# A long convolution's transform on one core: the product of u and D at the beginning of a block instead of behind the complex products

## The chip, the cores and the metric

The kernel runs on one core of one Trainium2 chip. The metric is the device time of one execution in microseconds (us); several executions are timed and the median counts. One further execution is profiled, and it has a time of its own. The engines have these names in the profile: PE is TensorE (PEld its weight loads), DVE is VectorE, ACT is ScalarE, POOL is GpSimd, and SP is the engine that here only issues transfers (DMA).

## The reference

Two independent layers read their own inputs, and their results stand side by side in the output (2048 x 2048, bf16). The left one is a recurrent attention with memory over 64 segments of 32 rows. The right one is a long convolution, and the change lies there:

```python
K = jnp.einsum('dn,dnl,dn->dl', Cc, P, dB).real          # P = exp(dt * A * l), complex
Kf = rfft(pad(K, L)); Uf = rfft(pad(u.T, L))             # L = 2048, transforms of length 4096, for each of 1024 channels
y = irfft(Uf * Kf)[:, :L].T + u * Dskip[None, None, :]
```

The last term, `u * Dskip`, is the product of the title; in the kernel it is one instruction for each sixteenth of the rows and channels.

## The kernel before

The work is in two parts. The convolution (`part_b`) runs first, up to about 593 us of the profile; the attention (`part_a`) follows. The second half of the convolution also loads the attention's weights, into memory that it gives up piece by piece.

Behind the tables, the convolution's transform is a loop of 16 blocks `b` (line 1526). Block `b` covers a quarter of the channels (`dq = b // 4`, DQ = 256 of them) and a quarter of the frequencies (`b % 4`). A block has these steps:

- VectorE, `times_u` (line 1380): four complex products of the spectrum of u, which SP has loaded as `uq` (the profile calls it wq), with the kernel's spectrum, which TensorE left in PSUM (`hps`). For each half n_ = 0, 1 it writes `Z` and then `Y`. `Zs` and `Yp` are one buffer each, used by every block.
- VectorE, `rotate` (lines 1383 and 1384): Y is completed from Z. From block 4 on there are two instructions for both halves (`whole`).
- VectorE, lines 1466 and 1467: `even` and `odd`, the sum and the difference of Y's halves. `even` is no buffer of its own, it is `Zs[:, 1]`, the Z of the second half; `odd` is called od in the profile.
- GpSimd, lines 1469, 1471 and 1472: from `even` (two instructions), and from `odd` (one each), the block's rows of `Bt`. In block 15 VectorE does lines 1471 and 1472.
- TensorE, `spectrum` (line 1224): the kernel's spectrum of block b + 1, 20 matmuls for each half. Three PSUM tiles go round, so that the second half's matmuls write the tile which the first half's products of block b have read.
- TensorE, from block 4 on, `inverses(b - 4, i)` (lines 1489 to 1521): the inverse transform of a pair of rows, 16 channel quarters in all, as matmuls of the matrices `MI` with `Bt`, and one matmul (line 1520) that adds the pair's product of u and D with the identity. ScalarE writes the result over the product (line 1521), and a transfer that ScalarE issues stores it (line 1493, issued during the inverses of the next pair).

The product itself is `skips(n_)` (line 1483), one VectorE instruction on 128 x 1024 bf16 (line 1486): `uu`, the pair's rows of u, times `Dsk`, D on all partitions, written over `uu`. The rows of pair n_ are loaded by `load_pair(n_)` (line 1481, SP), two blocks ahead of their use; pairs 0 and 1 are loaded in block 3. `load_u(b + 1)` (line 1215, SP) loads the spectrum of u for the next block, each half as soon as the products of that half are done.

`pointwise(b, ...)` is a generator: its first step issues `times_u`, its second the rest. Between the two stand, in the loop, the product, the loads and the spectra. Each engine runs its instructions in the order in which the program issues them; the engines wait for each other with semaphores. The loads and stores take their semaphores from a set of eight, in turn: a transfer is issued only when the one that last had its semaphore has landed. Which of them share one follows from the order that the framework gives the program.

The generator `residents` (line 1671) hands out the loads of the attention's weights: some in each block, and behind the loop the weights that go into the memory of `Zs`, `Yp`, the first `Bt` (given up by `ctx2.close()`, line 1591, ahead of the load of pair 15, line 1594), and of the matrices `MI`, one for each inverse that is done. The attention loads further pieces by itself, the first of them half of one query weight (a_half in the profile, line 352).

Of the kernel before, what the change touches and what calls it, by code (L numbers as in the profile page):

```python
# [711 lines left out]
def part_b(ctx, tc, u, A_re, A_im, B_re, B_im, C_re, C_im, log_dt, Dskip, out_b, ahead, copies, residents, first_state):  # L712
# [379 lines left out]
    def load_k(half, KT, lo):  # L1092
        n_ = KT.shape[1] // DH
        ks_ = [KT[:, DH * j:DH * j + DH] for j in range(n_)]
        for j, t_ in enumerate(ks_):
            c = lo + j
            src_ = Kp[half][8 * (c - 3):8 * (c - 2)] if c > 2 else Kx[half][4 * c:4 * c + 4, 8:40] if c < 2 else Kx[half][8:16, 8:40:2]
            sy.dma_start(out=t_, in_=src_ if c > 2 else src_.rearrange("i j g c -> i j (g c)"))
        return ks_
# [105 lines left out]
    def weighted(kc, n_, amp):  # L1205
        a_ = amp.rearrange("p (j q) -> p j q", j=3)[:, :, 256 * n_:256 * n_ + 256]
        g_ = G[kc][:, n_, 2:5].rearrange("p j s h f -> p j s (h f)")
        v.tensor_tensor(out=g_, in0=g_, in1=a_.unsqueeze(2).to_broadcast([128, 3, 2, 256]), op=ALU.mult)
# [4 lines left out]
    def load_u(b):  # L1213
        for n_ in range(2):
            sy.dma_start(out=uq[n_], in_=Ud[b % 4, b // 4][:, 2 * n_:2 * n_ + 2].rearrange("p a c d -> p (a c d)"))

    def spectrum(b, n_, outs, halves=(0, 1)):
        dq, kc = b // 4, b % 4
        KT = ks[dq // 2]
        d = slice(DQ * (dq % 2), DQ * (dq % 2) + DQ)  # L1220
        for half in halves:
            for cs in range(2):
                for j in range(5):
                    pe.matmul(outs[half][:, cs, :], lhsT=G[kc][:, n_, j, cs, half, :], rhs=KT[j][:, d], start=(j == 0), stop=(j == 4), skip_group_check=True)  # L1224
# [144 lines left out]
    def make(kc, n):  # L1369
        for _ in range(n):  # L1370
            next(made[kc])

    def halves():
        t_ = ps_e.tile([128, 2, 512], F32, name="pa", tag="pa")
        return [t_[:].rearrange("p h (c d) -> p h c d", c=2)]

    def times_u(s_, Y, Z, n_):
        us = uq[n_].rearrange("p (a c d) -> p a c d", a=2, c=2)
        for i, t_ in ((1, Z), (0, Y)):
            v.tensor_tensor(out=t_, in0=us[:, :, i, :].unsqueeze(2).to_broadcast([128, 2, 2, DQ]), in1=s_[n_][0], op=ALU.mult)  # L1380

    def rotate(Y, Z):
        v.tensor_tensor(out=Y[:, :, 0, :], in0=Y[:, :, 0, :], in1=Z[:, :, 1, :], op=ALU.subtract)
        v.tensor_tensor(out=Y[:, :, 1, :], in0=Y[:, :, 1, :], in1=Z[:, :, 0, :], op=ALU.add)
# [64 lines left out]
    def blocks(t_):  # L1449
        return t_.rearrange("p i c d -> p (i c) d")  # L1450

    def pointwise(b, s_):
        kc, Bt = b % 4, Bs[b // 4]
        Y = Yp[:] if b else first
        whole = b > 3
        if b:
            for n_ in range(2):
                times_u(s_, Y[:, n_], Zs[:, n_], n_)
                if n_ == 0 and not whole:
                    rotate(Y[:, n_], Zs[:, n_])  # L1460
        yield
        if whole:
            rotate(Y.rearrange("p n a c d -> p (n a) c d"), Zs[:].rearrange("p n a c d -> p (n a) c d"))
        elif b:
            rotate(Y[:, 1], Zs[:, 1])
        v.tensor_tensor(out=even, in0=Y[:, 0], in1=Y[:, 1], op=ALU.add)
        v.tensor_tensor(out=odd[:], in0=Y[:, 0], in1=Y[:, 1], op=ALU.subtract)
        for i, op in ((0, ALU.add), (1, ALU.subtract)):
            gp.tensor_tensor(out=Bt[:, kc, 0, i], in0=even[:, 0], in1=even[:, 1], op=op)
        eng, to = v if b == 15 else gp, blocks(Bt[:, kc, 1])  # L1470
        eng.tensor_tensor(out=to[:, 0:4:3], in0=odd[:, 0], in1=odd[:, 1, ::-1], op=ALU.add)
        eng.tensor_tensor(out=to[:, 2:0:-1], in0=odd[:, 0], in1=odd[:, 1, ::-1], op=ALU.subtract)
# [6 lines left out]
    def load_pair(n_, pool, bufs=4):  # L1479
        uu = held[n_] = pool.tile([128, 2, 2, DQ], BF16, name="uu", tag="uu", bufs=bufs)  # L1480
        sy.dma_start(out=uu[:].rearrange("p i a d -> p (i a) d"), in_=rows_of(u_v, n_))

    def skips(n_):
        d = slice(DQ * (n_ // 4), DQ * (n_ // 4) + DQ)
        uu = held[n_][:].rearrange("p i a d -> p (i a) d")
        v.tensor_tensor(out=uu, in0=uu, in1=Dsk[:, d].unsqueeze(1).to_broadcast([128, 4, DQ]), op=ALU.mult)

    def inverses(n_, i):
        while ended:
            ended.pop(0)()  # L1490
        inverse(n_ // 4, PAIRS[2 * n_ % 8 + i], held[n_][:, i])
        if i:
            ended.append(lambda: sc.dma_start(out=rows_of(out_v, n_), in_=held[n_][:].rearrange("p i a d -> p (i a) d")))
# [32 lines left out]
    for b in range(16):  # L1526
        dq = b // 4
        if b % 4 == 0:
            Bs[dq] = (bp0, bp)[dq % 2].tile([128, 4, 2, 2, 2, DQ], BF16, name="Bt", tag="B")
        points = pointwise(b, now)  # L1530
        next(points)
        if b >= 4:
            skips(b - 4)
        if 0 < b < 15:
            load_u(b + 1)
        if b >= 4:
            load_pair(b - 2, iv)
        if b == 3:
            v.tensor_scalar(out=ident[:], in0=ident[:], scalar1=float(PLEN / 2), scalar2=None, op0=ALU.mult)
            load_pair(0, iv)  # L1540
            load_pair(1, iv)
            ctx_p.close()
            ctx_k.close()
            ps_h = ctx.enter_context(tc.tile_pool(name="b_psh", bufs=3, space=PSUM))
            ps_y = ctx.enter_context(tc.tile_pool(name="b_psy", bufs=2, space=PSUM))
        if b == 0:
            now = nxt_
        elif b + 1 < 16:
            now = []
            for n_ in range(2):  # L1550
                if b < 3:
                    if n_:
                        next(points, None)
                    weighted(b + 1, n_, amps[b + 1])
                now.append(halves() if b < 3 else [ps_h.tile([128, 2, 2, DQ], F32, name="hps", tag="h")[:]])
                spectrum(b + 1, n_, [now[n_][0][:, half] for half in range(2)])
                if b == 1:
                    make(3, 7)
        next(points, None)
        if b < 4:  # L1560
            for i in (2 * b, 2 * b + 1):
                sy.dma_start(out=MI[i][:], in_=MId[2 * i:2 * i + 2].rearrange("c p a k q -> p c a k q"))
        if b == 2:
            rows4 = g0[0:4, 5120:6144]
            for i in range(4):
                for half in range(2):
                    sy.dma_start(out=rows4[i:i + 1, DH * half:DH * half + DH], in_=Kx[half][31:32, NF - 1].rearrange("i g c -> i (g c)"))
            sy.dma_start(out=w4, in_=u[0:4, :])
            gp.tensor_tensor(out=w4, in0=rows4[:, 0:D], in1=w4, op=ALU.mult)
            gp.memset(l4, 0.0)  # L1570
            gp.memset(l4[:, :, 127:128], float(PLEN / 2))
            gp.affine_select(out=l4[:, :, 127:128], in_=l4[:, :, 127:128], compare_op=ALU.is_ge, fill=0.0, base=0, pattern=[[1, 4], [0, 1]],
                             channel_multiplier=-1)
        for _ in range({1: 2, 2: 2, 3: 1, 4: 2, 5: 2, 6: 2, 7: 2, 11: 3, 12: 3, 13: 2, 14: 3, 15: 3}.get(b, 0)):
            next(resident)
        for _ in range(4 if b in (3, 4) else 0):
            second.pop(0)()
        if b == 5:
            ks.append(load_k(1, k1[:, 0:2560], 0))
        if b == 4:  # L1580
            state = first_state(g0[0:8, 5120:6144], iv.tile([128, 8, 24], BF16, name="xt0", bufs=1))
            next(state)
        if b == 10:
            state.send(ps_y.tile([128, 8, 128], BF16, name="yp", tag="yp")[:, :, 0:8])
        if b >= 4:
            for i in range(2):
                inverses(b - 4, i)
# [48 lines left out]
def kernel(  # L1636
# [90 lines left out]
    with ExitStack() as ctx_b:  # L1727
        part_b(ctx_b, tc, B_u[0], B_A_re, B_A_im, B_B_re, B_B_im, B_C_re, B_C_im, B_log_dt, B_Dskip, out_b, ahead, copies, residents, first_state)
# [37 lines left out]
```

## Time and profile before

| what | value |
|---|---|
| three executions | 1933.28, 1943.44, 1939.64 us; median 1939.64 |
| the profiled execution | 1942.13 us; span of its trace 1940.4 us |
| PE busy | 1783.4 us, 92% of the span |
| DVE busy | 1356.6 us, 70% |
| ACT busy | 918.6 us, 47% |
| POOL busy | 499.4 us, 26% |
| HBM read and written | 531.92 MB and 71.63 MB, 311 GB/s over the span |

By stage, busy time of the engines and mean share of the DMA engines:

| stage, us | length | PE | DVE | POOL | DMA share |
|---|---|---|---|---|---|
| 446 to 579, blocks 4 to 15 | 133 | 113.81 | 123.05 | 76.01 | 0.78 |
| 579 to 593, the last inverses | 14 | 13.31 | 2.25 | 8.62 | 0.98 |
| 593 to 640, the first segment and more | 47 | 27.83 | 16.39 | 2.81 | 1.02 |
| 640 to 1940, the other segments | 1300 | 1220.76 | 822.93 | 223.67 | 0.93 |

How to read it: the span is the time from the first to the last instruction of the profiled execution, and the execution's own time is 1.7 us longer. A busy share says nothing of what bounds a stage; that is seen where an engine waits and for whom. An instruction's length in the timeline includes the time in which it stands issued but is held up, so the same instruction can have two lengths. Instructions of one engine can overlap by some hundredths of a microsecond, so that the distance between starts is a better measure of what one costs than its length.

### The profile page before, as it was taken

The numbers are of one execution on the slowest core, as the hardware profiler recorded it, in microseconds if no ns is written. First come the engines' busy times: TensorE is split into PE (matmuls) and PEld (weight loads), VectorE is DVE, ScalarE is ACT, GpSimd is POOL, SyncE is SP. The second block draws the span as 40 slices with busy tenths as digits, with TensorE's granted clock in tenths as the row PEclk, the third lists the DMA queues.
The fourth block names the chain that finished last, engine by engine and source line by source line (L and its number), as shares of the span: only waits on it lengthen the run. The fifth ranks groups of instructions, "written<-read, shape, count | busy, mean of one in ns | idle before, by whom it ended". The sixth has DMA issues, their size and how long they took to land.

```text
span 1940.4 us, 73670 instructions
## 1 busy us (share of the span) xinstructions
PE 1783.4 (92%) x31563; PEld 1091.3 (56%) x31563; DVE 1356.6 (70%) x3357; ACT 918.6 (47%) x1654; POOL 499.4 (26%) x885
## 2 busy tenths in 40 slices
PE   8999999888886999999999999999999999999998
PEld 3666565556763555555555555555555555555554
DVE  8699999798992666676666666666667666766650
ACT  8799999850112343444444443434344444434420
POOL 2364545236561111111111111111112121111120
PEclk9999999868997999999999999999999999999999
DMA  7889898868699999999999999999999999999993
GB/s 222 250 238 282 238 282 250 216 193 249 196 294 373 334 336 341 339 342 342 340 339 349 344 335 340 346 339 344 331 349 343 343 343 357 336 337 339 345 338 96
DMA packets 341744, 594.21 MB, mean 306 GB/s; under 512 B 94100, under 2 KB 216476, under 8 KB 339368
## 3 DMA queue, kind: packets, MB, share of 16 engines
q1 hardware_dynamic: 297944, 534.99, 81.4%
q10 hardware_dynamic: 36816, 29.59, 4.8%
q0 software_dynamic: 6656, 24.92, 3.4%
q8 instruction: 247, 4.05, 0.8%
q14 instruction: 81, 0.66, 0.1%
HBM read 531.92 MB, written 71.63 MB: 311 GB/s over the span
## 4 chain that ended last, share of the span: by engine, by line
PE 46%; DMA 33%; DVE 12%; ACT 5%; issue 2%; POOL 1%; ACTq 0%; SPq 0%; POOLq 0%; DVEq 0%
PE acc L414 19%; DMA wst<-WD_v 12%; DMA wst<-WD_o 9%; PE pp L527 8%; DMA arena<-PKd 4%; PE pe L667 3%; DMA wst<-WD_k 3%; DMA wst<-WD_q 2%; PE tr L425 2%; PE pro L184 2%; PE yp L1508 1%; DVE nr L1269 1%; PE hps L1224 1%; PE pro L197 1%; PE pa L1224 1%
## 5 line engine op out<-in xcount | busy, mean ns | idle before, releaser
L414 PEld LDWEIGHTS <-a_hT 128*32 128x32 bf16 x12351 | 327.9, 96 | 331.5 <-issue 80.5
L420 ACT CAST arena<-acc 128x512 bf16<-128x512 f32 x384 | 224.8, 585 | 406.0 <-PE acc L414 336.8
L414 PE MATMUL acc<-wst,a_hT 128*32 128x512 bf16 x2308 | 230.5, 383 | 36.6 <-DMA wst<-WD_v 27.1
L527 PEld LDWEIGHTS <-arena 128*32 128x32 bf16 x8256 | 215.3, 96 | 76.7 <-issue 52.6
L428 POOL COPY arena<-arena 128x128 bf16<-128x128 bf16 x128 | 37.4, 292 | 707.1 <-DMA arena<-PKd 343.8
L335 DVE TENSOR_SCALAR arena<-keep 128x256 int32<-128x256 int32 x508 | 174.1, 394 | 26.6 <-PE acc L414 26.6
L414 PE MATMUL acc<-XM,a_hT 128*32 128x512 bf16 x2560 | 173.4, 381 | 0.0
L454 DVE TENSOR_REDUCE a_mx<-sc 128x4 f32<-128x160 f32 (+1 forms) x192 | 71.7, 374 | 80.9 <-PE sc L442 80.8
L197 PE MATMUL pro<-XM,wsl 128*128 128x512 bf16 x512 | 122.4, 382 | 4.0 <-DVE kst L206 2.2
L527 PE MATMUL pp<-W_o,arena 128*32 128x256 bf16 x3584 | 121.2, 273 | 1.3 <-issue 1.3
L414 PE MATMUL acc<-W,a_hT 128*32 128x512 bf16 x1536 | 119.7, 384 | 0.0
L544 DVE COPY arena<-tr 128x512 bf16<-128x512 bf16 x64 | 27.2, 424 | 129.2 <-PE tr L425 129.2
L458 ACT ACTIVATE sc<-sc 128x160 f32<-128x160 f32 (+1 forms) x192 | 63.9, 333 | 103.3 <-DVE sc L455 102.7
L462 DVE TENSOR_REDUCE a_mx<-sc 128x4 f32<-128x160 f32 (+1 forms) x192 | 72.8, 379 | 55.2 <-ACT sc L458 54.9
L489 POOL TENSOR_TENSOR arena<-arena,a_BD 128x128 bf16<-128x128 bf16 x128 | 51.0, 399 | 213.6 <-DVE arena L472 203.0
L1269 DVE TENSOR_SCALAR nr<-ptt 128x456 f32<-128x456 int16 x128 | 80.2, 627 | 30.4 <-PE ptt L1247 27.4
L1261 ACT ACTIVATE E<-pa 128x648 bf16<-128x648 f32 x128 | 87.6, 712 | 17.0 <-PE pa L1253 15.4
L414 PE MATMUL acc<-wq,a_hT 128*32 128x512 bf16 x1024 | 92.3, 383 | 0.0
L527 PE MATMUL pp<-wst,arena 128*32 128x256 bf16 x1536 | 76.2, 274 | 17.5 <-DMA wst<-WD_o 16.5
L414 PE MATMUL acc<-g,a_hT 128*32 128x512 bf16 x1024 | 91.2, 380 | 0.0
L623 ACT CAST arena<-pp 128x128 bf16<-128x128 f32 x64 | 17.0, 265 | 155.7 <-DVE arena L623 155.7
L513 ACT CAST arena<-pv 128x512 bf16<-128x512 f32 (+1 forms) x128 | 61.3, 479 | 60.3 <-PE pv L499 33.3
(342 smaller groups left out, 4001.7 us busy)
## 6 DMA issues: line engine op xcount, KB each, us to landing
wst<-WD_v SPq DMA_DIRECT2D x256, 512.0 KB
wst<-WD_k SPq DMA_DIRECT2D x192, 512.0 KB
wst<-WD_o SPq DMA_DIRECT2D x192, 512.0 KB
wst<-WD_q SPq DMA_DIRECT2D x128, 512.0 KB
Ud<-ux POOLq DMA_DIRECT2D x16, 1024.0 KB, 8.9
wq<-Ud SPq DMA_DIRECT2D x32, 512.0 KB
wsl<-in_A_Wk_dram SPq DMA_DIRECT2D x16, 512.0 KB
wsl<-in_A_Wv_dram SPq DMA_DIRECT2D x16, 512.0 KB
```

Of the source, the lines that this page charges most:

```text
L197: nc.tensor.matmul(a[:], lhsT=w[:, kc, 128 * j:128 * j + 128], rhs=xTl[:, kc, :, :].rearrange("p s k -> p (s k)"), start=(kc == 0), stop=( ...
L335: nc.vector.tensor_scalar(out=out.bitcast(I32), in0=in_.bitcast(I32), scalar1=0, scalar2=None, op0=ALU.bitwise_or)
L414: nc.tensor.matmul(a[32 * g:32 * g + 32, o_:o_ + rhs.shape[1]], lhsT=hT[:, kc, :], rhs=rhs, start=(kc == 0), stop=(kc == KC - 1), tile_pos ...
L420: nc.scalar.copy(out=q, in_=a[:])
L454: nc.vector.tensor_reduce(out=m_, in_=x, axis=AX.X, op=ALU.max)
L458: nc.scalar.activation(out=flat(sc, i), in_=flat(sc, i), func=ACT.Exp, scale=scale)
L462: nc.vector.tensor_reduce(out=m_, in_=x, axis=AX.X, op=ALU.add)
L513: copy(out=o[:, i:i + n], in_=p[:, i:i + n, :].rearrange("p a (g q) -> p a g q", g=4))
L527: nc.tensor.matmul(po[32 * qt:32 * qt + 32, o_:o_ + rhs.shape[1]], lhsT=oT[:, h % 4, (h % 16) // 4, :], rhs=rhs, start=False, stop=(h == 3 ...
L667: nc.tensor.matmul(pe[n][:], lhsT=left[2 * b + hi // 16][:, 128 * (hi % 16):128 * (hi % 16) + 128], rhs=wo[u][:, 1024 * hh + 512 * n:1024 ...
L1261: sc.activation(out=T["E", r, e // 4][:, lo:lo + 8 * NE].rearrange("p (i c) -> p i c", i=2), in_=T.pop(("p", r, e))[:, :, 0:4 * NE], func= ...
L1269: v.tensor_scalar(out=T["n", r, e // 4][:, lo:lo + 8 * NT], in0=T.pop(("t", r, e))[:, 0:8 * NT].bitcast(I16)[:, 0:16 * NT:2], scalar1=floa ...
```

## The change

`skips(b - 4)`, the product, is called before the generator's first step instead of behind it. On VectorE the twelve products of blocks 4 to 15 are thus issued ahead of the four instructions of `times_u`, which is directly behind `odd` of the block before (in block 11 one short copy stands between). The four products of the last pairs, behind the loop, stay.

```diff
         if b % 4 == 0:
             Bs[dq] = (bp0, bp)[dq % 2].tile([128, 4, 2, 2, 2, DQ], BF16, name="Bt", tag="B")
+        if b >= 4:
+            skips(b - 4)
         points = pointwise(b, now)
         next(points)
-        if b >= 4:
-            skips(b - 4)
         if 0 < b < 15:
             load_u(b + 1)
```

## The prediction

> **What bounds the kernel now.** I read the page's slices first, then the chain of waits, then the timeline of single engines in the stretch that the change touches.
>
> ```profile
> DVE  8699999798992666676666666666667666766650
> ```
>
> Slices are 48.5 us. The change lies in the sixteen blocks of the transform; those it touches (4 to 15) run from 446 to 579 us, slices 10 to 12, where VectorE has 8, 9, 9 tenths. Behind them come 64 segments of attention (593 us to the end), which it does not touch. One block, on VectorE and GpSimd:
>
> ```profile
> 503.74 1.22 DVE L1467 TENSOR_TENSOR od<-y 128x1024 f32<-128x1024 f32 x1
> 504.87 1.22 DVE L1380 TENSOR_TENSOR z<-wq,hps 128x1024 f32<-128x1024 f32 x1
> 506.00 1.22 DVE L1380 TENSOR_TENSOR y<-wq,hps 128x1024 f32<-128x1024 f32 x1
> 507.34 1.22 DVE L1380 TENSOR_TENSOR z<-wq,hps 128x1024 f32<-128x1024 f32 x1
> 508.48 1.21 DVE L1380 TENSOR_TENSOR y<-wq,hps 128x1024 f32<-128x1024 f32 x1
> 509.61 0.72 DVE L1486 TENSOR_TENSOR uu<-uu,Dsk 128x1024 bf16<-128x1024 bf16 x1
> 510.25 1.21 DVE L1383 TENSOR_TENSOR y<-y,z 128x1024 f32<-128x1024 f32 x1
> ...
> 513.77 1.22 DVE L1467 TENSOR_TENSOR od<-y 128x1024 f32<-128x1024 f32 x1
> ```
> ```profile
> 503.96 3.35 POOL L1469 TENSOR_TENSOR Bt<-z 128x512 bf16<-128x512 f32 x2 [4.22 <-PE yp L1520]
> 507.27 1.27 POOL L1471 TENSOR_TENSOR Bt<-od 128x512 bf16<-128x512 f32 x1
> ```
>
> Columns: start, length, engine, line. VectorE has no gap: the block lasts 10.03 us, start to start, and that is its own work plus one wait. Starts inside it lie 1.13 apart; only the second z lies 1.34 behind y, because its buffer is the one that L1469 reads, and L1469 ends at 507.31. TensorE waits 1.25 us a block for y, so it is not the bound. Earlier, blocks 6 and 7 wait for a load (3.52 and 3.44 us before z at 471.71 and 485.03).
>
> What the end of the blocks sets is the loading of the weights of the next part:
>
> ```profile
> 574.32 3.87 POOL L1469 TENSOR_TENSOR Bt<-z 128x512 bf16<-128x512 f32 x2 [4.16 <-DVE z L1466]
> ```
> ```profile
> 574.40 4.19 SPq L1481 DMA_DIRECT2D uu<-in_B_u_dram  x2
> 578.68 0.46 SPq L268 DMA_DIRECT2D W_v<-in_A_Wv_dram  x1
> ```
> ```profile
> 578.00:580.00 2.00, 2.00 (x18) 1.55 (x16) 2.00 (x4) 0.00 (x0) 1.99 (x7) 1.00 0.34 98
> ```
> ```profile
> 610.59 0.61 PE L414 MATMUL acc<-a_half,a_hT 128*32 128x512 bf16 x2 [14.01 <-DMA a_half<-in_A_Wq_dram]
> ```
>
> The load of pair 15 goes into memory that block 15's last GpSimd additions give up at 578.19; SP stands there, the DMA engines run dry (0.34 busy, 98 GB/s), and all weights behind follow at about full share until TensorE, idle for 14 us, gets a_half at 610.59. So the end of L1469 in block 15 is what to follow.
>
> **The change part by part.** The built programs hold the same instructions on each engine; on VectorE twelve products L1486 move from behind y to behind the od of the block before. The order on TensorE, ScalarE, GpSimd and SP stays, and the product issues no transfer. Behind it on VectorE now stand z and y, for which TensorE's next spectrum and SP's load of u wait. What some transfers wait for changes as well (below).
>
> *The product beside GpSimd.* In its old place GpSimd is almost done (L1472 ends at 509.77); in the new one GpSimd is in L1469. The trace has a near twin: L1208, also a bf16 product of two SBUF tensors, stands right behind od in blocks 1 and 2.
>
> ```profile
> 429.52 0.95 DVE L1208 TENSOR_TENSOR XM<-XM,wq 128x1536 bf16<-128x1536 bf16 x1
> ...
> 432.85 1.22 DVE L1467 TENSOR_TENSOR od<-y 128x1024 f32<-128x1024 f32 x1
> 433.98 2.02 DVE L1208 TENSOR_TENSOR XM<-XM,wq 128x1536 bf16<-128x1536 bf16 x1
> 435.93 1.21 DVE L1380 TENSOR_TENSOR z<-wq,pa 128x1024 f32<-128x1024 f32 x1
> ```
> ```profile
> 433.01 4.13 POOL L1469 TENSOR_TENSOR Bt<-z 128x512 bf16<-128x512 f32 x2 [6.95 <-DVE z L1466]
> ```
>
> Alone, L1208 holds VectorE 0.86 us (429.52 to 430.38); behind od, with L1469 running, 1.95, and L1469 takes 4.13 in place of about 3.4. The same at 419.93. I read it so: GpSimd, held off while od reads SBUF, goes next; VectorE waits for that one instruction; GpSimd's second waits for VectorE. That is 1.08 us on top. The product alone takes 0.62 (start to start), so 1.70. The rule for this is in the Trainium skill, SBUF — State Buffer, section "SBUF: two separate sides": the port pair shared by the two engines is a lock, and the loser is blocked for the other's whole instruction. With GpSimd's 1.27 us (L1471) as that wait, the sum would be about 1.5 us higher; I keep the 1.08 of the row. The page does not say who goes first when both wait; the two rows say GpSimd.
>
> Per block: od to z +1.70; behind y the product's slot goes, and L1383 follows y directly, 1.25 later (423.00 to 424.25) instead of 1.77: -0.52; the second z no longer waits for GpSimd, whose 4.1 us end before it is due 5.1 us behind od: -0.21. Together +0.97, 10.03 to 11.00. Bounds: -0.11 without any port wait; +2.4 if both L1469 instructions (2.5 us) went first. The value nearest to the twin stays.
>
> *Where it counts.* Blocks 6 and 7 hide it in their load waits. From z of block 7 (485.03) on nothing does: block 8's z comes 1.70 - 0.52 = 1.18 later, seven more blocks add 7 x 0.97 = 6.79, and in block 15 itself 0.52 + 0.21 come off before L1466 ends. L1469 of block 15 ends 7.2 us later, at 585.4. Bounds for this term, by those of a block: -1.4 and +19.
>
> *Block 4.* The product there reads pair 0, whose load SP issues at 443.46; its place is now 446.6 instead of 452.70. When it lands no row says: between the two. GpSimd's L1469 ends at 449.0; I take the product to run then, z at 449.7 in place of 447.47. TensorE, the store of pair 1 (468.22) and with it SP, which waits for that store before it loads u for block 7 (475.10), come up to 3 us later. The DMA share is about 1.0 from 470 to 482, so much of that is a place in a queue: 0 to 3, I take 1.0.
>
> *TensorE's wait for the last product.* At 566.0 TensorE waits 4.79 us for product 11, then runs at half clock (14 matmuls in 3.19 us, elsewhere 1.69). That wait goes; the next is for the last additions of block 15 (VectorE, 578.7 before, 585.9 now), nearly as long, and half clock follows it: TensorE's last inverses and their stores leave about 2.7 us later still. Neither is ahead of the weights by itself.
>
> *Semaphores shared by loads and stores.* In the changed program SP's second weight into freed matrix space waits for the store of pair 12, the sixth for that of pair 14, a_half for that of pair 15. Before, the third waited for that of pair 12: the store left at 582.48, SP went on at 593.96, 11.5 us. Behind a gate at 585.9 eight weights (4 MB) are 12 to 13 us of transfer at 320 GB/s to 340; the store of pair 12, issued near 591, lands about 599 to 602. So the queue can run dry twice, by 0 to 3 us each: I take 2.3 in all.
>
> Sum: 7.2 + 1.0 + 2.3 = 10.5. The attention that follows counts nothing: it is the same program, 1347 us behind 593. Against the profiled execution (span 1940.4, its own time 1942.13): 1952.6. That run is 2.5 us above the median 1939.64, so on the scale of the median 1950.1, 0.54% up.
>
> **The rivals**, on the median's scale. *No port wait* (other side): the 2.02 us of L1208 come from its own operands, one of which ScalarE had just written, and the product runs in 0.62 beside GpSimd. For it: od keeps its 1.22 us while L1469 is under way. Against: two rows of 2.02 beside 0.95. Price: z of block 8 +0.10, 7 x -0.11, -0.73: -1.4 us, 1938.2; it decides from a product of under about 0.8 us. *Absorbed*: blocks are slower, but the weights behind the gate do not shift by all of it and no queue runs dry, +4, 1943.6. For: the share is above 1.0 from 570 to 574. Against: 0.34 at 578. *Cool clock*: TensorE's wait per block grows from 1.25 to 2.2 us; if that halved its clock for some 5.5 us (as behind the 4.38 us at 474), its 8.8 us would be 11.5, 0.5 a block more than VectorE's, +3.5, 1953.6. Against: 1.83 us at 487.44 did not. The Trainium skill, TensorE: Matmul & The Clock Gate, section "What's actually happening", has the clock fall after an idle window of about 3.4 us; by it the clock stays, and the trace so far agrees. *Deep drain*: the stores hold SP longer, 7 us of dry queue, 1955.
>
> **How the numbers follow.** Forecast 0.55, no port wait 0.12, absorbed 0.15, cool clock 0.06, deep drain 0.12. Half a per cent is 9.7 us, about what a measurement of this kernel can tell from no change. The forecast's own range is 1946 to 1953, with two thirds of it above that bound: slower 0.37 + 0.06 + 0.12 = 0.55; faster 0.03, from the first rival with the scatter of runs (1933 to 1943); within 0.42. The range leaves out half of the first rival and the tail of the last: 1940 to 1957.
>
> **What would show it.** L1486 of blocks 5 to 15 at about 1.75 us instead of 0.71, L1469 pairs at 4 us; blocks of 11.0 us; the second z 1.13 behind y; no wait of TensorE for L1486; pair 15's load near 585.5; a_half near 621. I am wrong if L1486 stays at 0.7, if blocks stay at 10, or if a_half comes before 614 although blocks are 11 us long.

## The result and the profile after

| | before | changed |
|---|---|---|
| median of 22 runs each | 1938.09 us (1924.99 to 1947.90) | 1946.62 us (1939.51 to 1961.71) |
| ratio, 95% interval | | 1.0045 [1.0029, 1.0061], which is +8.7 us (5.6 to 11.8) |
| profiled execution, its span | 1942.13, 1940.4 us | 1942.59, 1940.9 us |
| VectorE busy | 1356.6 us | 1369.4 us |

The changed kernel is slower by 0.45%. The two profiled executions alone would not show it, their spans differ by 0.5 us: what was lost before the attention happens to be balanced by a shorter attention in this one execution (from a_half, below, to the end 1329.8 us before, 1321.6 changed; in the kernels of the experiments it scatters alike, from 1320 to 1330, but for the two with stores on GpSimd's queue). So the stages are compared in the traces, and the times by the medians.

One block of the changed kernel, in the timeline of VectorE and then of GpSimd (start, length, engine, line):

```profile
504.19 1.22 DVE L1467 TENSOR_TENSOR od<-y 128x1024 f32<-128x1024 f32 x1
505.33 1.76 DVE L1486 TENSOR_TENSOR uu<-uu,Dsk 128x1024 bf16<-128x1024 bf16 x1
507.00 1.21 DVE L1380 TENSOR_TENSOR z<-wq,hps 128x1024 f32<-128x1024 f32 x1
508.14 1.21 DVE L1380 TENSOR_TENSOR y<-wq,hps 128x1024 f32<-128x1024 f32 x1
509.27 1.21 DVE L1380 TENSOR_TENSOR z<-wq,hps 128x1024 f32<-128x1024 f32 x1
...
515.18 1.22 DVE L1467 TENSOR_TENSOR od<-y 128x1024 f32<-128x1024 f32 x1
```
```profile
504.42 3.80 POOL L1469 TENSOR_TENSOR Bt<-z 128x512 bf16<-128x512 f32 x2 [4.71 <-DVE z L1466]
```

The same product that took 0.72 us behind y takes 1.76 behind od. From its start to that of z pass 1.67 us, where the product alone needs 0.62. The second z now follows y at the common distance of 1.13, so it waits for nothing. From od to od the block lasts 10.99 us, 10.03 before. VectorE's 12.8 us of additional busy time are for the most part these lengths: eleven products are longer by about 1.05 and that of block 4 by 0.5, 12.1 in all.

At the end of the blocks, in the timelines of GpSimd, SP and TensorE:

```profile
581.26 3.85 POOL L1469 TENSOR_TENSOR Bt<-z 128x512 bf16<-128x512 f32 x2 [4.66 <-DVE z L1466]
```
```profile
584.02 1.49 SPq L1481 DMA_DIRECT2D uu<-in_B_u_dram  x2
585.60 1.40 SPq L268 DMA_DIRECT2D W_v<-in_A_Wv_dram  x3
...
593.91 8.16 SPq L268 DMA_DIRECT2D W<-in_A_Wv_dram  x4
```
```profile
619.30 0.61 PE L414 MATMUL acc<-a_half,a_hT 128*32 128x512 bf16 x2 [13.57 <-DMA a_half<-in_A_Wq_dram]
```

L1469 of block 15 ends at 585.11, 6.92 us later than before. SP stands at the load of pair 15 until then (its issue is the second of the group that begins at 584.02). The weights follow, and TensorE gets a_half at 619.30, 8.71 us later than before. In the table of windows (length, busy time of PE, PEld, DVE, ACT and POOL, clock, DMA share, GB/s) the DMA engines run dry ahead of that gate, as they did before:

```profile
582.00:584.00 2.00, 0.51 (x4) 0.39 (x4) 1.97 (x3) 0.00 (x0) 2.00 (x2) 1.00 0.37 120
```

### The profile page after: what moved, and what is told of

It reads as the page before. It is cut to its first block, busy times and chain, and to the rows that moved or that the text cites. A ratio compares the mean times of both kernels' runs of the same rounds, so it can differ in the third digit from the quotient of the medians.

```text
span 1940.9 us, 73678 instructions
## 1 busy us (share of the span) xinstructions
PE 1786.6 (92%) x31563; PEld 1095.1 (56%) x31563; DVE 1369.4 (71%) x3357; ACT 919.5 (47%) x1654; POOL 503.9 (26%) x885
## 4 chain that ended last, share of the span: by engine, by line
PE 46%; DMA 31%; DVE 15%; ACT 4%; issue 3%; SPq 0%; POOL 0%; DVEq 0%; POOLq 0%; ACTq 0%
PE acc L414 22%; DMA wst<-WD_v 11%; DMA wst<-WD_o 10%; PE pp L527 8%; PE pe L667 3%; DMA wst<-WD_k 3%; DMA wst<-WD_q 2%; PE tr L425 2%; DVE nr L1269 2%; PE pro L184 2%; DMA out_dram<-uu 2%; DMA arena<-PKd 1%; DVE y L1380 1%; DVE z L1380 1%; PE pa L1224 1%
## 5 line engine op out<-in xcount | busy, mean ns | idle before, releaser
L335 DVE TENSOR_SCALAR arena<-keep 128x256 int32<-128x256 int32 x508 | 174.0, 393 | 29.1 <-PE acc L414 29.0
L527 PE MATMUL pp<-wst,arena 128*32 128x256 bf16 x1536 | 76.4, 274 | 20.3 <-DMA wst<-WD_o 16.9
L425 PEld LDWEIGHTS <-arena 128*128 128x128 bf16 x1024 | 57.8, 98 | 54.8 <-issue 26.3
```

The lines of the kernel that those rows point to most:

```text
L335: nc.vector.tensor_scalar(out=out.bitcast(I32), in0=in_.bitcast(I32), scalar1=0, scalar2=None, op0=ALU.bitwise_or)
L425: nc.tensor.transpose(out=p[:, hl, :, :].rearrange("p a b -> p (a b)"), in_=q[:, 128 * hl:128 * hl + 128], identity=ident[:])
L527: nc.tensor.matmul(po[32 * qt:32 * qt + 32, o_:o_ + rhs.shape[1]], lhsT=oT[:, h % 4, (h % 16) // 4, :], rhs=rhs, start=False, stop=(h == 3 ...
```

## The experiments

Below, the gate is the end of the last GpSimd pair on z in block 15, and "a_half" the start of TensorE's first product with it. The columns before the ratio come from one profiled execution of each kernel; the blocks start up to 5.6 us later in one than in another (VectorE's sum in the block ahead of block 4 starts between 444.29 and 449.89, in the two kernels with the stores on GpSimd's queue up to 451.32), so the gate is best read with some microseconds of play and the distance from gate to a_half with less.

| kernel | product | block, us | gate | a_half | between | ratio to before, 95% |
|---|---|---|---|---|---|---|
| before | 0.72 | 10.03 | 578.19 | 610.59 | 32.4 | |
| changed | 1.76 | 10.99 | 585.11 | 619.30 | 34.2 | 1.0045 [1.0029, 1.0061] |
| late only | 1.76 | 10.99 | 585.56 | 619.76 | 34.2 | 1.0044 [1.0018, 1.007] |
| early only | 0.71 from block 8 | 10.04 | 578.24 | 609.91 | 31.7 | 0.9995 [0.9973, 1.0018] |
| no GpSimd | 0.68 | 9.91 | 576.75 | 611.27 | 34.5 | one run |
| between the halves | 0.73 | 9.96 | 580.65 | 614.86 | 34.2 | 1.0 [0.998, 1.0019] |
| between, late | 0.73 | 9.96 | 577.06 | 611.10 | 34.0 | 0.9992 [0.9972, 1.0012] |
| reversed | 1.76 | 10.99 | 585.30 | 619.76 | 34.5 | 1.0053 [1.003, 1.0077] |
| strided | 2.44 | 11.63 | 596.43 | 630.93 | 34.5 | 1.0071 [1.0045, 1.0096] |
| stores on GpSimd | 1.76 | 10.99 | 589.22 | 618.39 | 29.2 | 1.0101 [1.0076, 1.0126] |
| between and stores | 0.74 | 9.97 | 581.92 | 610.98 | 29.1 | 1.007 [1.0047, 1.0093] |

### Which blocks count

```diff
-        if b >= 4:
+        if b >= 8:
             skips(b - 4)
         points = pointwise(b, now)
         next(points)
+        if 4 <= b < 8:
+            skips(b - 4)
```

and the mirror image, `if 4 <= b < 8` ahead and `if b >= 8` behind. Expected of the first:

> The product stands at the beginning of the block from block 8 on; in blocks 4 to 7 it stays behind the complex products, as before the change. Theory (the product waits for GpSimd's L1469, and this counts only from block 8 on): L1486 takes 1.75 us in blocks 8 to 15 and 0.7 in blocks 4 to 7, the end of L1469 in block 15 stays at 585.1 +-0.4, TensorE's first product on a_half starts at 619 +-1, time 1946 +-3, as with the whole change. Rival 1 (the early blocks carry the loss too, each block alike): four of twelve products are back in place, a third of the loss goes: end of L1469 at 582.8. Rival 2 (the loss is scatter of the attention): a_half as with the whole change, but the ratio to before within 0.2% of 1.

And of the second:

> The product stands at the beginning of the block in blocks 4 to 7 alone; from block 8 on it stays behind the complex products. Theory: L1486 still takes 1.7 us in blocks 5 and 6 or 7, but the complex products of block 7 start at 485.0, held by their load, the end of L1469 in block 15 is at 578.2 +-0.4 as before the change, a_half at 610.6 +-1, time 1938 +-3, ratio 1.000. Rival 1 (each block alike): end of L1469 at 580.5. Rival 2 (the loss is scatter of the attention): the same times as the late half of the change.

Late only is the whole loss (1944.81 us median against 1938.02), early only is none of it (1936.52). In the timelines of early only, VectorE and then GpSimd:

```profile
481.14 1.76 DVE L1486 TENSOR_TENSOR uu<-uu,Dsk 128x1024 bf16<-128x1024 bf16 x1
485.55 1.22 DVE L1380 TENSOR_TENSOR z<-wq,hps 128x1024 f32<-128x1024 f32 x1 [2.65 <-DMA wq<-Ud]
```
```profile
574.37 3.87 POOL L1469 TENSOR_TENSOR Bt<-z 128x512 bf16<-128x512 f32 x2 [4.15 <-DVE z L1466]
```

The product of block 7 is as long as any, but behind it VectorE waits 2.65 us for a load, as it did before the change (3.44): the longer product takes up time in which VectorE would have waited. Late only has the gate of the whole change to half a microsecond, and a_half too. Neither rival, a loss shared alike by all blocks or a loss that is only scatter of the attention, fits the pair.

### What the product waits for

```diff
+        if b in (4, 8, 12):
+            gp.memset(Bs[dq][:], 0.0)
         if b >= 4:
             skips(b - 4)
...
+        if 4 <= b < 15:
+            return
         for i, op in ((0, ALU.add), (1, ALU.subtract)):
             gp.tensor_tensor(out=Bt[:, kc, 0, i], in0=even[:, 0], in1=even[:, 1], op=op)
```

> The whole change; GpSimd's operations L1469 and L1471/L1472 of blocks 4 to 14 are left out, and the matrix Bt is filled with zeros once at the beginning of blocks 4, 8 and 12 (so the last three quarters of the inverse transform are not computed). Theory (the product waits for GpSimd): L1486 takes 0.7 +-0.05 in every block but 4, 8 and 12, where it lies beside the fill, and a block takes 9.9 +-0.1 us. Rival (the length is the product's own at this place, by its operands or by the write of the difference ahead of it): L1486 stays at 1.75 in all blocks.

With the same place on VectorE, but GpSimd's additions gone, VectorE's timeline is

```profile
494.42 0.68 DVE L1488 TENSOR_TENSOR uu<-uu,Dsk 128x1024 bf16<-128x1024 bf16 x1
...
504.37 0.68 DVE L1488 TENSOR_TENSOR uu<-uu,Dsk 128x1024 bf16<-128x1024 bf16 x1
```

0.68 us and a block of 9.91: the length belongs to GpSimd's additions, not to the operands or the place. Only the product of block 4 is long (1.81 us from 449.83); there GpSimd's first addition from `odd` of block 3, which is still made, starts at the same time (449.82, 1.26 us). One thing came out otherwise than expected: the product of block 8, the first line above, does lie beside the fill, and is not held up by it:

```profile
493.96 6.92 POOL L1533 MEMSET Bt<- 128x8192 bf16 x1 [32.86 <-PE yp L1510]
```

This is GpSimd's timeline. The fill runs from 493.96 to 500.88, as long as another fill (6.93 us from 452.71). The product of block 12 lies beside its fill in the same way (0.68 us from 534.21, the fill 6.92 us from 533.73). So this fill, which only writes SBUF, and the product do not hold each other up; the additions, which read it, and the product do.

### Which operations wait

Two other access patterns for the same product, first reversed, then in steps of two:

```diff
-        v.tensor_tensor(out=uu, in0=uu, in1=Dsk[:, d].unsqueeze(1).to_broadcast([128, 4, DQ]), op=ALU.mult)
+        v.tensor_tensor(out=uu[:, :, ::-1], in0=uu[:, :, ::-1], in1=Dsk[:, d][:, ::-1].unsqueeze(1).to_broadcast([128, 4, DQ]), op=ALU.mult)
```
```diff
+        uu, Dd = uu.rearrange("p n (d e) -> p n e d", e=2), Dsk[:, d].rearrange("p (d e) -> p e d", e=2)
+        v.tensor_tensor(out=uu, in0=uu, in1=Dd.unsqueeze(1).to_broadcast([128, 4, 2, DQ // 2]), op=ALU.mult)
```

> The whole change, but the product runs through each row from its last element to its first on all three operands, so that the same product is made by another access pattern. Theory (the product waits for GpSimd because of the fast form in which it runs, 0.7 us for 1024 bf16 per partition against 1.2 for float32): if the reversed pattern makes it run at the slower rate, L1486 takes 1.2 +-0.1 without a wait, a block takes 10.5 +-0.1, end of L1469 in block 15 at 581 +-0.5. Rival A (every VectorE operation on bfloat16 waits here, whatever its rate): L1486 at 2.2 or more, block 11.5. Rival B (the reversed pattern keeps the fast form): L1486 at 1.75 and all else as with the change.

Reversed, the product keeps its rate (0.69 us for the last one, with no addition beside it) and everything is as with the change, 1.76 us and blocks of 10.99. That run tells nothing apart.

> The whole change, but the product takes the even elements of each row first and then the odd ones on all three operands, so every access steps by two bfloat16 elements; the same product by another access pattern. Theory (the product waits for GpSimd because of the fast form in which it runs): if the stride takes the fast form away, L1486 lasts 1.2 +-0.1 (the float32 operations of the same 1024 elements take 1.21) and doesn't wait; a block takes 10.5 +-0.1, end of L1469 in block 15 at 581.5 +-0.7 and the time 1942 +-3: an operation that is slower by itself costs less. Rival A (every VectorE operation on bfloat16 waits at this place): L1486 at 2.2 or more, blocks 11.5, end of L1469 at 589. Rival B (the stride keeps the fast form): 1.75, as with the change.

The stride does take the fast rate away, and the product waits all the same. In the timelines of VectorE and GpSimd:

```profile
512.17 2.44 DVE L1487 TENSOR_TENSOR uu<-uu,Dsk 128x1024 bf16<-128x1024 bf16 x1
514.51 1.20 DVE L1380 TENSOR_TENSOR z<-wq,hps 128x1024 f32<-128x1024 f32 x1
...
596.90 4.95 DVE L1487 TENSOR_TENSOR uu<-uu,Dsk 128x1024 bf16<-128x1024 bf16 x4
```
```profile
511.26 4.44 POOL L1469 TENSOR_TENSOR Bt<-z 128x512 bf16<-128x512 f32 x2 [4.74 <-DVE z L1466]
```

Four products behind the last block, with no additions beside them, take 4.95 us, 1.24 each. Behind od one takes 2.34 from start to start, 1.10 more, the same wait as the fast one's 1.05. GpSimd's pair grows with the product's own length: 3.33 to 3.42 us beside none (before), 3.77 to 3.87 beside the product of 0.62, 4.42 to 4.52 beside that of 1.24. So the two engines take turns: od first, then GpSimd's first addition while VectorE waits, then the product while GpSimd's second addition waits. My theory, that it is the fast form that waits, fell; rival A's numbers came (2.44, blocks 11.63), apart from the gate, which is later still, for the most part by the late start of the blocks in this execution (5.6 us). What the product shares with od and not with z is that both inputs lie in SBUF: z reads one of them from PSUM and keeps its 1.21 us beside L1469. The Trainium skill, SBUF — State Buffer, section "SBUF: two separate sides", says that a VectorE operation with two SBUF inputs and a GpSimd operation that reads SBUF exclude each other at the shared pair of ports, and that the one that starts first holds it for its whole instruction. The turns of od, additions and product agree with it, and so does the fill, which reads nothing and runs beside the product.

### A place without the wait

```diff
             for n_ in range(2):
                 times_u(s_, Y[:, n_], Zs[:, n_], n_)
+                if n_ == 0 and b >= 4:
+                    skips(b - 4)
```

with the call ahead of the block taken out.

> The product stands between the two halves of the complex products, behind y of the first half and ahead of z of the second; everything else is as before the change. Theory: GpSimd's pair L1469 (3.8 us from the sum) overlaps it by little or nothing (it ends about 3.8 us into a block, the product would begin at 1.1+1.2+1.1 = 3.4), so L1486 takes 0.7 to 1.1, z of the second half no longer waits for GpSimd, blocks take 9.9 to 10.2, end of L1469 in block 15 between 577 and 579.5, a_half at 609 to 612, ratio 0.998 to 1.001. Rival (any place ahead of the last complex product costs, since the matrix engine gets the block later): end of L1469 later than 581.

VectorE's wait is gone, as expected. In VectorE's timeline of this kernel and then in GpSimd's:

```profile
510.10 0.73 DVE L1488 TENSOR_TENSOR uu<-uu,Dsk 128x1024 bf16<-128x1024 bf16 x1
```
```profile
506.93 3.35 POOL L1471 TENSOR_TENSOR Bt<-z 128x512 bf16<-128x512 f32 x2 [3.70 <-PE yp L1522]
510.24 1.73 POOL L1473 TENSOR_TENSOR Bt<-od 128x512 bf16<-128x512 f32 x1
```

Here the product starts at 510.10, GpSimd's next addition at 510.24, and it is GpSimd that waits: 1.73 us in place of 1.27. VectorE's block is 9.96 us, shorter than before. But the gate was expected by 579.5 and a_half by 612; they came at 580.65 and 614.86. In this execution the load for block 6 held z for 6.20 us, where it was 3.52 before: SP had stood at a transfer that shares its semaphore with the store of pair 0, which landed late (issued 460.65, SP went on at 465.90; before 459.61 and 463.13). The same place from block 8 on alone (`b >= 8` there, blocks 4 to 7 as before):

> The product stands between the two halves of the complex products from block 8 on, and behind them in blocks 4 to 7, as before the change. Theory (the later gate of the run with the product between the halves in all blocks came from blocks 6 and 7, where its loads were late, and not from the place itself): blocks 9.96 as there, z of block 7 at 485.0 +-0.5, end of L1469 in block 15 at 577.6 +-0.5, a_half at 609 to 611, ratio 0.998 to 1.000. Rival (the place itself delays the gate): end of L1469 at 580.6.

The gate is at 577.06, within the theory's 577.6 +-0.5, and blocks are 9.96 us, so from block 8 on the place itself delays nothing. (z of block 7 came at 484.44, a little ahead of its range.) a_half comes at 611.10 all the same, no earlier than before, because the way from the gate to it is longer; the next part is about that. Both versions take the same time as before within 0.2% (1.0 and 0.9992): a gain of one microsecond at the gate isn't seen in the time. Why the load of block 6 was late in the one execution was not followed further.

### From the gate to a_half

```diff
         if i:
-            ended.append(lambda: sc.dma_start(out=rows_of(out_v, n_), in_=held[n_][:].rearrange("p i a d -> p (i a) d")))
+            if n_ < 12:
+                ended.append(lambda: sc.dma_start(out=rows_of(out_v, n_), in_=held[n_][:].rearrange("p i a d -> p (i a) d")))
+            else:
+                for h in range(2):
+                    ended.append(lambda h=h: gp.dma_start(out=rows_of(out_v, n_)[:, 2 * h:2 * h + 2], in_=held[n_][:, h]))
```

> The whole change; in addition the stores of pairs 12 to 15 leave from GpSimd's queue, each in two parts, and no longer take a turn among the eight semaphores that SP's loads use. Theory (a part of the delay behind the late load of pair 15 is SP's queue waiting for stores that share its semaphores): end of L1469 in block 15 stays at 585.1 +-0.4, the weights behind it leave SP earlier, a_half is used at 616 to 618 instead of 619.3, ratio to before 1.003. Rival (the delay is the late load alone, and the memory's own rate sets the rest): a_half at 619.3 +-0.5, ratio 1.0045.

> The product between the halves from block 8 on, and the stores of pairs 12 to 15 from GpSimd's queue. Theory: both gains add, end of L1469 at 577.6, a_half at 606 to 609, ratio to before 0.996 to 0.999. Rival (attention's start doesn't follow a_half, or GpSimd's queue holds the stores and its own attention work): ratio 1.000 or above.

The column "between" of the table falls into three groups. Without the stores in the turn it is 29.1 and 29.2. In before and early only it is 32.4 and 31.7, and in the seven others 34.0 to 34.5. The groups follow the order that the programs give the eight semaphores: in before and early only the third weight behind the gate waits for the store of pair 12, in the seven others already the second. In all nine that weight leaves SP 15.2 to 16.9 us behind the gate; where it is the second, one weight more is still to come (512 KB, an estimated 1.5 us at the 340 GB/s of these stretches). The mean of the seven less that of the two is 34.30 - 32.04 = 2.26 us.

The 29 us are not a matter of the semaphores alone. By the profile's count of transfers 10.5 MB move between the gate and a_half in those two kernels, 11.1 to 11.6 MB in the nine others, since five of the eight half stores leave only when a_half is already in use. At 330 to 360 GB/s, the rates of these stretches, the difference of about 0.9 MB is an estimated 2.5 us, half of what separates 34.3 and 29.1; no run tells the two parts from each other.

The time, though, is worse than before by 20 us and 14 us; in the first kernel, 8.7 of them are the change's own. In the timeline of TensorE in the kernel with the change and these stores, then of GpSimd, and then of SP:

```profile
618.39 0.61 PE L414 MATMUL acc<-a_half,a_hT 128*32 128x512 bf16 x2 [9.37 <-DMA a_half<-in_A_Wq_dram]
632.20 0.33 PE L439 MATMUL sc<-arena 128*32 128x40 bf16 x16 [9.31 <-POOL arena L428]
```
```profile
631.11 0.73 POOL L1497 DMA_DIRECT2D out_dram<-uu  x1 [1.80 <-issue]
631.85 0.30 POOL L428 COPY arena<-arena 128x128 bf16<-128x128 bf16 x1
```
```profile
613.44 0.38 SPq L340 DMA_DIRECT2D wst<-WD_q  x1
633.49 1.41 SPq L268 DMA_DIRECT2D W_o<-in_A_Wo_dram  x3
```

GpSimd issues the eight half stores one behind the other, from 602.65 to 631.84, and a copy that the first segment of the attention needs stands behind them: TensorE waits 9.31 us for it. SP stands longer still: behind 613.82 it issues nothing until 633.49, because its next load, W_o, waits for the landing of all eight half stores (in the trace, the semaphores that it waits for are theirs). Meanwhile the DMA engines are nearly idle, a share of 0.19 from 620 to 634, where it is 1.05 in the changed kernel. From a_half to the end these two kernels take 1346 and 1341 us, the others 1320 to 1330; how the two waits share in that was not separated.

The theories of the two runs missed. The gate came at 589.22 and 581.92, where 585.1 and 577.6 were expected (the blocks started 3.6 and 7.0 us later than before in these two executions, but late starts are seen elsewhere too), and a_half at 618.39 and 610.98, behind both ranges. Only the distance shrank, in the first kernel by more than expected. "Both gains add" missed in the time as well: 1953.3 us. The wait for stores is real, and this way out of it costs more than it does.

## Why the prediction was right

The forecast was +10.5 us and 1950.1; measured are 1946.62 and +8.5 between the medians (ratio +8.7, 5.6 to 11.8). The mechanism is the one named; its sum was 2 us too large, and the terms show where. With an interval from 5.6 to 11.8 the time alone says little of a sum of 10.5; the terms are what bears it out. Whether the loss is above the half per cent that the chances were divided at stays open: 0.45%, and the interval reaches to both sides.

- **The product beside GpSimd.** 1.70 from od to z was forecast from the twin L1208; it is 1.67. Blocks of 11.00 are 10.99, the second z lies 1.13 behind y. The run without GpSimd's additions shows that they are the cause, and the strided run that the wait has nothing to do with the product's rate. That is why the twin's 1.08 could be carried over from an operation half as long again: it is what is left of GpSimd's addition, and not a share of the product. The rival *No port wait* is out.
- **Where it counts.** z of block 7 starts at 485.02, before at 485.03. From there the gate was to come 7.2 us later; it came 6.92 later. (The prediction has this gate at 585.4 and, where it sums up the weights, at 585.9; nothing hangs on the difference.) Late only and early only bear out the split at block 8.
- **Block 4.** This term, 1.0 of a range from 0 to 3, was nothing. The product waited for its load, z came at 449.70 exactly as taken, but the load waits ahead of blocks 6 and 7 swallowed it:

```profile
448.58 1.20 DVE L1486 TENSOR_TENSOR uu<-uu,Dsk 128x1024 bf16<-128x1024 bf16 x1 [1.69 <-DMA uu<-in_B_u_dram]
449.70 1.21 DVE L1380 TENSOR_TENSOR z<-wq,hps 128x1024 f32<-128x1024 f32 x1
...
485.02 1.22 DVE L1380 TENSOR_TENSOR z<-wq,hps 128x1024 f32<-128x1024 f32 x1 [2.28 <-DMA wq<-Ud]
```

The path that was feared did come: the store of pair 1 left at 470.35 instead of 468.22, and SP issued the load of u for block 7 at 480.35 instead of 475.10. The load landed at the same time all the same, beside a DMA share of 0.33 from 478 to 480, where it was 1.05 before. Nothing in the traces says that the two must cancel; that the term was nothing and not up to 3 us is chance, as far as is known.

- **Semaphores shared by loads and stores.** Taken as 2.3; in the changed kernel's one profiled execution it is 34.19 - 32.40 = 1.8, over the groups of kernels 2.26. One wait was not foreseen: already the first weight leaves 8.80 us behind the gate (593.91 - 585.11) and 6.54 before (584.73 - 578.19), since it waits for the third of the W_v loads in place of the second. The whole turn is one transfer tighter, not only where stores stand. That one does not seem to cost anything, though: in the strided kernel the first weight leaves 6.69 us behind the gate, nearly as early as before, and the way to a_half is 34.5 us all the same. What is left is the wait that was forecast, the second weight's for the store.
- **TensorE's wait for the last product.** The wait of 4.79 us is gone, as said; TensorE waits 2.71 for L1469 and 2.23 for a later product instead (so "no wait of TensorE for L1486" holds for the moved products alone). Half clock follows, as forecast, and the stores of pairs 13 and 14 leave 2.2 us later behind the gate than before (9.45 and 13.69 us in place of 7.22 and 11.46); 2.7 was the forecast.
- **The sum.** Without the term of block 4 it is 9.5; a_half moved by 8.71 and the medians by 8.5. That fits an attention that passes on all of it, but one profiled execution each can't show it, with 1320 to 1330 us from a_half to the end. *Absorbed* (+4) is out by late only's gate and a_half; *Deep drain* (7 us of dry queue) by 1.8.
- **Cool clock.** Half right, without price. TensorE's wait grew to 2.21 us, and its clock did fall in some blocks, so the prediction's reading that the clock stays was wrong. But it was at half for 3.4 us, not 5.5, and the blocks stayed at 10.99; see below.

## What to carry to other kernels

An instruction that moves to a place where nothing waits for it can still be held by the engine beside it: look at which GpSimd and VectorE operations read two SBUF tensors side by side, find a twin in the trace that already stands in such a place, and take its row as the price. Then follow the delay to what the stage hands on; cover that exists in some blocks (here a load wait of 2 us and more) takes the price there and nowhere else. And a change in the order of instructions can also change which transfers share a semaphore: here worth about 2 us, without a single transfer being moved.

## What was not expected of the hardware

TensorE's clock fell behind waits of 2.21 us, in some blocks and not in others of the same kernel. In TensorE's timeline of the changed kernel, the same 20 matmuls behind the same wait:

```profile
553.35 2.36 PE L1224 MATMUL hps<-k,XM 128*128 128x256 bf16 x20 [2.21 <-DVE y L1380]
...
564.34 3.76 PE L1224 MATMUL hps<-k,XM 128*128 128x256 bf16 x20 [2.21 <-DVE y L1380]
```

and in windows of 3.41 us, the one with most of the first wait, the one with the second, and the one behind it (the column behind the busy times is the clock):

```profile
551.45:554.86 3.41, 1.51 (x14) 1.37 (x15) 3.41 (x4) 0.00 (x0) 3.17 (x3) 1.00 1.02 355
561.69:565.10 3.41, 1.21 (x12) 0.84 (x10) 3.41 (x4) 0.00 (x0) 3.41 (x3) 1.00 0.83 292
565.10:568.51 3.41, 3.41 (x18) 2.42 (x17) 3.38 (x4) 0.00 (x0) 0.51 (x1) 0.50 0.82 232
```

The clock is at half from 565.10 to 568.51, 3.41 us, and the group takes 1.4 us longer. It cost nothing here, since VectorE sets the block (10.99 us before and behind it). The trace also shows why one wait cools the clock and the other does not. The clock's changes lie 3.41 us or a multiple of it apart (520.73, 524.14, 565.10, 568.51 in these blocks). In the stretch of 3.41 us ahead of the fall at 565.10 TensorE is busy for 1.21 us, so that the whole wait of 2.21 lies in it; ahead of the fall at 520.73 it is the same. The wait ahead of 553.35 lies across two such stretches, TensorE is idle for 1.90 us in the later one, and the clock stays at full until 565.10. The Trainium skill, TensorE: Matmul & The Clock Gate, section "What's actually happening", gives an idle window of about 3.4 us that runs freely. The trace agrees with a window that runs freely, but not with one that must be idle throughout: 2.2 us of 3.41 were enough here.

The other surprise is who waits. Beside the same additions GpSimd waits for od (its pair takes 3.4 us where two instructions alone take 2.5), VectorE's product then waits 1.05 us for GpSimd, GpSimd's second addition waits for the product, and a fill that only writes waits for nobody. Each of these three is held until the one of the other engine that began before it has ended, whatever its own rate: the product waits 1.05 us, what is left of an addition of 1.26.
